# One GpSimd subtraction per pair of score rows instead of two, in a fused top-k attention and feed-forward kernel

## The chip, the core and the metric

The kernel runs on one core of a Trainium2 chip. A core has five engines with instruction streams of their own: TensorE (PE in the profile, with its weight loads as PEld), VectorE (DVE), ScalarE (ACT), GpSimd (POOL) and SyncE (SP, which here only issues transfers). Each works its stream in order, and semaphores tie the streams together. The metric is the device time of one execution in microseconds (us), as the median of several runs. Beside it stands one profiled execution, whose span and rows are those of the profile.

## The reference

Eight batches of eight heads, 576 positions, head size 64. Of each score row only the 32 largest entries are kept; the rest get no weight. The attention's output, as 4608 rows of 512, goes through a feed-forward pair of matrices with a leaky activation between them.

```python
scores = scale * np.matmul(q, k.transpose(0, 1, 3, 2))
kth = np.partition(scores, -top_k, axis=-1)[..., -top_k:-top_k + 1]   # top_k = 32
mask = scores >= kth
scores = np.where(mask, scores, -1000000000.0)
...
attn = np.exp(scores)
attn = attn / (np.sum(attn, axis=-1, keepdims=True) + 1e-09)
return np.matmul(attn, v).astype(np.float32)
...
h = x @ w_in
g = np.maximum(h, 0.0) + alpha * np.minimum(h, 0.0)
return (g @ w_out).astype(np.float32)
```

## The kernel before

Heads are taken two at a time, which makes 32 pairs of heads. The unit of the attention is a *duo*: two blocks of 128 score rows (one per head of a pair, or the last 64 positions of two pairs put together), so a tile of 128 partitions by 2 rows by 576 scores. There are 144 duos, 18 per batch. In this document a "row" of a duo is one of its two 576-wide halves.

A duo passes through these steps, each a function in the kernel:

- `st_qk` (PE) makes the scores in PSUM, and `st_exit` (ACT, one copy of 1152 elements) brings them to SBUF as the tile `s_sb`.
- `dve_slot` (DVE) takes the eight largest of each of six groups of 96 columns (`up`, `small`), and every second slot turns those of two duos into a bound for each row (`threshold_steps`, tiles `bot`, `neg`, `p`).
- `st_count` (ACT) computes for each of the two rows the sign of bound minus score (tile `sg`), and adds the signs up, which tells how many scores lie above the bound.
- `st_y` (POOL) multiplies scores by signs, one instruction of 576 elements per row (tile `y`). Scores above the bound change their sign, so the eight largest of `y` (DVE, `row`) are the candidates next below it. From the count and the candidates `pick_steps` (DVE) selects the 32nd largest score (`KT`, in tile `KZ`).
- `st_relu` (ACT and POOL) masks: ACT computes for each row Relu(2^60 x (kth - score)) into the tile `r`, which is zero where the score is kept and huge elsewhere, and POOL subtracts `r` from `s_sb` in place.
- `st_exp` (ACT, one instruction of 1152 elements, tile `w`) takes the exponential of both rows, and SP issues the transposing transfer to `wT`; `st_av` (PE) multiplies by the values; `norm_a` and `norm_b` (DVE) divide by the sum.

The feed-forward runs between these steps in small units (`h_pe`, `h_relu`, `o_pe`, `o_act`), and so do loads, the transposition of `q` and `k` on PE (copied out as `qkT` by ACT or DVE), and the casts of `v` on POOL (`cast_v`, tile `v`: two of 128x256 and one of 64x128 per pair of heads).

The order of each engine is written out by hand. The main loop has one *slot* per duo number n, and a table of lags says which duo each step takes in slot n: the count takes duo n-2, the mask duo n-4, Exp duo n-5, the values duo n-8 (from the thirteenth on n-7), the exit copy duo n+1. `Ordered` (line 21) keeps every engine's instructions in the order in which the loop makes them, apart from small DVE instructions. So in slot n ACT works: two Sign (duo n-2), Exp (duo n-5), sometimes a copy `o_sb` of a finished output, two Relu (duo n-4), the exit copy (duo n+1), sometimes a copy `qkT`. POOL works: two products `y` (duo n-2), two subtractions (duo n-4), sometimes a cast. The Exp of slot n+1 reads what slot n's subtractions wrote; the row maxima on DVE read what `y` wrote.

The tiles `sg` and `r` share a ring of three buffers, `s_sb` has six and `y` two. The first 140 duos are masked by `st_relu`; the last four use another way (`st_all`, `st_mask`) behind the loop, without a subtraction on POOL.

`st_relu` is called twice in a row, for rows 0 and 1, in the main loop (lines 744 to 746).

Of the kernel before, what the change touches and what calls it, by code (L numbers as in the profile page):

```python
# [12 lines left out]
ALU = mybir.AluOpType  # L13
# [46 lines left out]
def fast_path(tc, q, k, v, moe_w_in, moe_w_out, moe_alpha, out, flag):  # L60
# [11 lines left out]
    PE, ACT, DVE, POOL, SP = (  # L72
        Ordered(tc, e) for e in (nc.tensor, nc.scalar, nc.vector, nc.gpsimd, nc.sync)
    )
# [18 lines left out]
    with ExitStack() as ctx:  # L93
# [297 lines left out]
        def st_relu(n, i):  # L391
            s = T["s", n]
            if i == 0:
                T["r", n] = two.tile([128, 2, S], BF16, name="r", tag="sg", bufs=3)
            r = T["r", n]
            ACT.activation(r[:, i, :], s[:, i, :], AF.Relu, bias=KT[:, 2 * n + i:2 * n + i + 1], scale=-BIG)
            POOL.tensor_tensor(s[:, i, :], s[:, i, :], r[:, i, :], ALU.subtract)

        def st_exp(n):
            w = ws[n % 4]  # L400
# [313 lines left out]
        for n in range(ND):  # L714
# [29 lines left out]
            for m in duos_at("relu", n):  # L744
                st_relu(m, 0)
                st_relu(m, 1)
# [412 lines left out]
```

## Time and profile before

| what | value |
|---|---|
| median of 3 runs | 825.62 us (824.25 to 825.81) |
| the profiled execution's own time | 823.81 us |
| its span | 821.6 us |
| PE / DVE / ACT / POOL busy | 733.2 / 757.5 / 762.9 / 745.4 us |
| products `y` on POOL | 288, mean 1278 ns |
| subtractions on POOL | 280, mean 1277 ns |
| Relu `r` on ACT | 280, mean 769 ns |

A row of the groups reads: line, engine, operation, tile written and tiles read, shapes, count; then the busy time in us and the mean of one in ns; then the idle time of the engine just before these instructions and what ended it. Nearly all instructions carry line 32, the helper in `Ordered` that makes them, so the tiles name them. In rows in order of time the first number is the start in us from the span's start, the second the time from the first start to the last end of the instructions that the row merges (xcount); neighbours on one engine overlap at their ends, so starts stand a little closer than durations. A row of a window gives its bounds and length, the busy times of PE, PEld, DVE, ACT and POOL with their counts, then the granted TensorE clock, the share of the DMA engines and GB/s.

### The profile page before, as it was taken

How to read it: one execution, taken by the hardware profiler on the slowest of the kernel's cores; microseconds unless marked ns; L12 is line 12 of the kernel's file. 1: busy time of each engine (PE TensorE's matmuls, PEld its weight loads, DVE VectorE, ACT ScalarE, POOL GpSimd, SP SyncE). 2: the span in 40 equal slices, each digit the busy share in tenths (PEclk: the TensorE clock that was granted, in tenths of full speed). 3: DMA queues.
4: the chain of work that ended last, by engine and by line, in shares of the span. 5: the costliest groups of instructions: out<-in, count | busy, mean ns of one | idle time of the engine just before them, and what ended most of it. 6: DMA issues, size and time to landing. Idle time of an engine off the chain costs nothing.

```text
span 821.6 us, 17795 instructions
## 1 busy us (share of the span) xinstructions
PE 733.2 (89%) x5343; PEld 423.0 (51%) x5418; DVE 757.5 (92%) x3471; ACT 762.9 (93%) x1257; POOL 745.4 (91%) x701
## 2 busy tenths in 40 slices
PE   8888898989989899898989898898989899999886
PEld 5333444555545555455555454555545555565554
DVE  4999997999999999999999999999999999999951
ACT  4999997999999999999999999999999999999931
POOL 1899997999998999999999999999999998999920
PEclk9999998999999999999999999999999999999999
DMA  6699986556555656566566566566667654444461
GB/s 143 167 179 185 176 131 137 105 124 122 124 122 121 120 103 143 109 136 122 114 131 131 111 98 135 123 130 128 113 123 132 120 110 103 91 98 83 89 101 50
DMA packets 344328, 100.24 MB, mean 122 GB/s; under 512 B 338192, under 2 KB 338208, under 8 KB 344224
## 3 DMA queue, kind: packets, MB, share of 16 engines
q1 hardware_dynamic: 341152, 91.90, 57.1%
q0 software_dynamic: 1872, 6.82, 3.6%
q8 instruction: 45, 0.74, 0.4%
q14 instruction: 59, 0.48, 0.2%
q10 hardware_dynamic: 1200, 0.30, 0.2%
HBM read 36.71 MB, written 9.44 MB: 56 GB/s over the span
## 4 chain that ended last, share of the span: by engine, by line
DVE 46%; POOL 16%; PE 15%; ACT 15%; issue 5%; DMA 3%; SPq 0%; DVEq 0%; ACTq 0%; POOLq 0%
DVE small L32 14%; DVE p L32 12%; DVE up L32 8%; POOL y L32 8%; POOL s_sb L32 7%; DVE gT L32 5%; PE ps_sc L32 4%; ACT sg L32 4%; ACT r L32 4%; ACT s_sb L32 3%; PE pz L32 3%; PE ph L32 3%; ACT w L32 2%; DVE qkT L32 2%; PE xo L32 2%
## 5 line engine op out<-in xcount | busy, mean ns | idle before, releaser
L32 POOL TENSOR_TENSOR y<-s_sb,sg 128x576 f32<-128x576 f32 x288 | 362.6, 1278 | 33.5 <-ACT sg L32 33.1
L32 POOL TENSOR_TENSOR s_sb<-s_sb,r 128x576 f32<-128x576 f32 x280 | 352.1, 1277 | 7.6 <-ACT r L32 7.1
L32 ACT ACTIVATE sg<-s_sb,p 128x576 bf16<-128x576 f32 x288 | 221.3, 773 | 8.6 <-DVE p L32 7.1
L32 DVE MAX8 up<-s_sb 128x8 f32<-128x96 f32 x864 | 213.4, 247 | 10.1 <-ACT s_sb L32 10.1
L32 DVE MAX8 p<-y 128x8 f32<-128x576 f32 x288 | 215.4, 749 | 6.5 <-POOL y L32 5.8
L32 DVE MAX8 small<-s_sb 128x8 f32<-128x96 f32 x864 | 217.6, 252 | 0.0
L32 PE MATMUL ps_sc<-qkT 64*128 64x512 f32 (+2 forms) x768 | 185.2, 572 | 18.8 <-ACT s_sb L32 18.7
L32 ACT ACTIVATE r<-s_sb,KZ 128x576 bf16<-128x576 f32 x280 | 201.0, 769 | 0.3 <-DVE KZ L32 0.3
L32 ACT COPY s_sb<-ps_sc 128x1152 f32<-128x1152 f32 x144 | 159.0, 1104 | 12.8 <-PE ps_sc L32 12.3
L32 ACT ACTIVATE w<-s_sb 128x1152 bf16<-128x1152 f32 x140 | 161.7, 1155 | 1.0 <-POOL s_sb L32 0.8
L32 PE MATMUL ph<-xT,w_in_b 128*128 128x256 bf16 (+1 forms) x1472 | 151.4, 251 | 5.9 <-ACT qkT L32 2.8
L32 PEld LDWEIGHTS <-w_in_b 128*128 128x128 bf16 x1472 | 120.6, 98 | 49.2 <-issue 10.4
L32 PE MATMUL pz<-w_out_b,gT 128*128 128x512 bf16 x517 | 134.6, 379 | 8.1 <-issue 6.3
L32 PE MATMUL xo<-v,wT 128*128 128x65 bf16 (+1 forms) x1560 | 123.8, 199 | 5.6 <-DMA wT<-w 3.9
L32 PEld LDWEIGHTS <-wT 128*128 128x128 bf16 (+3 forms) x1600 | 97.9, 100 | 39.7 <-DMA wT<-w 8.6
L32 DVE TENSOR_SCALAR gT<-ph 128x512 bf16<-128x512 f32 x136 | 91.9, 676 | 11.4 <-PE ph L32 11.4
L32 PEld LDWEIGHTS <-gT 128*128 128x128 bf16 x576 | 55.8, 98 | 69.8 <-issue 14.6
L32 PEld LDWEIGHTS ps_sc<-kd,qkT 128*128 128x128 f32 x256 | 38.5, 190 | 99.6 <-issue 96.1
L32 PEld LDWEIGHTS ps_sc<-qkT 64*128 64x128 f32 (+1 forms) x768 | 55.8, 170 | 62.7 <-issue 29.3
L32 PE MATMUL ps_sc<-kd,qkT 128*128 128x128 f32 x256 | 63.1, 329 | 1.1 <-DMA kd<-qkT 1.1
L32 PE MATMUL rest<-idle 128*128 128x512 bf16 x196 | 49.8, 380 | 7.3 <-DVE gT L32 5.4
L32 ACT ACTIVATION_READ_ACCUMULATOR sg<-s_sb,p 128x1 f32 x288 | 55.7, 194 | 0.0
(66 smaller groups left out, 580.0 us busy)
## 6 DMA issues: line engine op xcount, KB each, us to landing
k_st<-in_k_dram SPq DMA_DIRECT2D x64, 128.0 KB, 2.9
v_st<-in_v_dram SPq DMA_DIRECT2D x64, 128.0 KB, 2.7
q_st<-in_q_dram SPq DMA_DIRECT2D x62, 128.0 KB, 2.8
out_dram<-o_sb SPq DMA_DIRECT2D x31, 256.0 KB, 2.5
w_st<-in_moe_w_out_dram POOLq DMA_DIRECT2D x4, 1024.0 KB, 6.8
wT<-w SPq DMA_TRANSPOSE x144, 3.5
w_in_b<-in_moe_w_in_dram POOLq DMA_DIRECT2D x4, 512.0 KB, 6.5
k_st<-in_k_dram SPq DMA_DIRECT2D x32, 32.0 KB, 2.5
```

What stands on the lines that cost most here:

```text
L32: ins = self.tc.keep_in_program_order(f(*a, **kw))
```

## The change

Both Relu stay as they are. The subtraction is no longer issued once for each row but once behind the second Relu, over the whole tile of 128 x 2 x 576, which is contiguous and so one run of 1152 elements per partition. It reads what both Relu wrote and stands in POOL's order where the second subtraction stood. The products `y` remain one instruction per row, and the lags stay.

```diff
         def st_relu(n, i):
...
             ACT.activation(r[:, i, :], s[:, i, :], AF.Relu, bias=KT[:, 2 * n + i:2 * n + i + 1], scale=-BIG)
-            POOL.tensor_tensor(s[:, i, :], s[:, i, :], r[:, i, :], ALU.subtract)
+            if i:
+                POOL.tensor_tensor(s, s, r, ALU.subtract)
```

## The prediction

> **What bounds the kernel now.** I read the page first (busy shares, groups, the shares of the chain of waits), then the table of waits, then one stretch of 18 slots as a window, then the instructions of that stretch in order of time.
>
> ```profile
> span 821.6 us, 17795 instructions
> PE 733.2 (89%) x5343; PEld 423.0 (51%) x5418; DVE 757.5 (92%) x3471; ACT 762.9 (93%) x1257; POOL 745.4 (91%) x701
> DVE 46%; POOL 16%; PE 15%; ACT 15%; issue 5%; DMA 3%; SPq 0%; DVEq 0%; ACTq 0%; POOLq 0%
> L32 POOL TENSOR_TENSOR y<-s_sb,sg 128x576 f32<-128x576 f32 x288 | 362.6, 1278 | 33.5 <-ACT sg L32 33.1
> L32 POOL TENSOR_TENSOR s_sb<-s_sb,r 128x576 f32<-128x576 f32 x280 | 352.1, 1277 | 7.6 <-ACT r L32 7.1
> ```
>
> Four engines lie between 89 and 93% busy and the chain is spread over all of them, so no engine alone is the bound. The subtraction (280 times, 1277 ns) waited 7.1 us in all for ACT's Relu.
>
> ```profile
> 517.63:610.97 93.34, 84.11 (x605) 48.98 (x612) 92.39 (x431) 93.00 (x154) 92.87 (x85) 1.00 0.61 122
> ```
>
> This is a stretch of 18 slots, from one slot's subtraction to the same place 18 slots on. Busy times are PE, weight load, DVE, ACT, POOL: of 93.34 us ACT is idle 0.34, POOL 0.47, DVE 0.95. Whatever makes one of the three wait in this stretch has almost nothing to hide in, and the granted TensorE clock (1.00) is whole.
>
> ```profile
> ACT w L32 <- POOL s_sb L32: 0.8, 3, 0.5
> DVE p L32 <- POOL y L32: 5.8, 11, 1.2
> ```
>
> So far ACT's Exp (`w`) has almost never waited for the subtraction: 0.8 us, three times.
>
> The loop that matters runs over two engines. ACT works through Exp of duo n-5, perhaps a copy `o_sb`, two Relu of duo n-4, the exit copy of duo n+1, perhaps a copy `qkT`, two Sign of the next slot, next Exp. That next Exp needs this slot's subtraction. A slot with no extra copy, on ACT:
>
> ```profile
> 525.72 1.15 ACT L32 ACTIVATE w<-s_sb 128x1152 bf16<-128x1152 f32 x1
> 526.77 1.42 ACT L32 ACTIVATE r<-s_sb,KZ 128x576 bf16<-128x576 f32 x2
> 528.11 1.09 ACT L32 COPY s_sb<-ps_sc 128x1152 f32<-128x1152 f32 x1
> 529.11 0.77 ACT L32 ACTIVATE sg<-s_sb,p 128x576 bf16<-128x576 f32 x1
> ...
> 530.63 1.15 ACT L32 ACTIVATE w<-s_sb 128x1152 bf16<-128x1152 f32 x1
> ```
>
> Exp to Exp is 4.91 us. The second Relu ends 2.47 us after Exp began (526.77 + 1.42 - 525.72), and 2.44 us of ACT work follow before the next Exp. The first Relu ends some 0.67 us ahead of the second (1.42 less its own 0.77, which is how far two starts stand apart). POOL in the same time:
>
> ```profile
> 522.81 2.51 POOL L32 TENSOR_TENSOR s_sb<-s_sb,r 128x576 f32<-128x576 f32 x2
> 525.28 2.50 POOL L32 TENSOR_TENSOR y<-s_sb,sg 128x576 f32<-128x576 f32 x2
> 527.75 2.51 POOL L32 TENSOR_TENSOR s_sb<-s_sb,r 128x576 f32<-128x576 f32 x2
> 530.21 0.39 POOL L32 CAST v<-v_st 128x256 bf16<-128x256 f32 x1
> 530.57 2.52 POOL L32 TENSOR_TENSOR y<-s_sb,sg 128x576 f32<-128x576 f32 x2
> ...
> 540.80 0.28 POOL L32 CAST v<-v_st 64x128 bf16<-64x128 f32 x1
> 541.05 2.51 POOL L32 TENSOR_TENSOR y<-s_sb,sg 128x576 f32<-128x576 f32 x2
> ```
>
> A pair takes 2.47 us from start to start and 2.51 to its own end; a large cast adds 0.36, a small one 0.25. The subtraction at 527.75 starts 0.44 us before the second Relu ends (528.19). That head start is what the change forbids.
>
> **The change, part by part.** 140 pairs of subtractions become 140 single ones of 1152 elements on POOL, at the place of the second; PE, DVE, ACT and SP keep their work and order, and no DMA moves.
>
> *The wait it adds.* The one instruction needs both Relu, so it starts at the later of the end of `y` and the second Relu's end. Behind it on POOL stand the casts and the next `y`, for which DVE's row maxima wait; ACT's Exp waits for the subtraction itself, and behind Exp everything on ACT. The two semaphore delays show where one engine did stand waiting:
>
> ```profile
> 552.62 0.57 ACT L32 COPY o_sb<-pz 128x512 f32<-128x512 f32 x1
> 553.08 1.45 ACT L32 ACTIVATE r<-s_sb,KZ 128x576 bf16<-128x576 f32 x2
> 553.95 2.52 POOL L32 TENSOR_TENSOR s_sb<-s_sb,r 128x576 f32<-128x576 f32 x2 [0.41 <-ACT r L32]
> ...
> 422.78 2.51 POOL L32 TENSOR_TENSOR s_sb<-s_sb,r 128x576 f32<-128x576 f32 x2
> 425.32 1.16 ACT L32 ACTIVATE w<-s_sb 128x1152 bf16<-128x1152 f32 x1 [0.16 <-POOL s_sb L32]
> ```
>
> The first Relu of 553.08 ends near 553.86 and the subtraction begins 0.08 to 0.09 later (I use 0.08); a subtraction ending at 425.29 lets Exp begin 0.03 later. `o_sb` adds 0.46 us between Exp and Relu (552.62 to 553.08).
>
> *What it saves.* One start less per duo. Its fixed price is not in the trace for this shape. From below: nothing. The nearest row for a flat operation is memset on POOL:
>
> ```profile
> 1.25 0.93 POOL L32 MEMSET kd<- 128x128 f32 x6
> 2.91 0.47 POOL L32 MEMSET v<- 128x10 bf16 x8
> ...
> L32 POOL MEMSET kd<- 128x128 f32 x6 | 0.9, 204 | 0.0
> L32 POOL MEMSET v<- 128x10 bf16 x8 | 0.5, 173 | 0.0
> ...
> L32 POOL CAST v<-v_st 128x256 bf16<-128x256 f32 x8 | 3.2, 398 | 0.0
> L32 POOL CAST v<-v_st 64x128 bf16<-64x128 f32 x4 | 1.2, 290 | 0.0
> L32 ACT COPY qkT<-tps 128x512 f32<-128x512 f32 x4 | 2.3, 584 | 0.0
> L32 ACT COPY o_sb<-pz 128x512 f32<-128x512 f32 x4 | 2.3, 568 | 0.0
> ```
>
> Without the last one's own time, memsets of 128 elements start (0.93 - 0.20) / 5 = 0.15 us apart and those of 10 elements (0.47 - 0.17) / 7 = 0.04 apart: nearly all of the 0.04 is fixed. From above, the casts: 0.36 for 256 elements and 0.25 for 128 leave 0.25 - 128 x 0.11/128 = 0.14 fixed, with an access pattern of several levels. The subtraction is flat, like the memset, so I take 0.04: the merged instruction holds POOL 2.43 us and ends 2.47 after its start.
>
> A rule of the Trainium skill bears on this term. "GPSIMD Engine Reference", section 3.1, gives 4497 ns for a two-input operation of 2048 elements and a floor of about 2.5 cycles per element at 1.2 GHz. By that floor (an estimate) 576 elements are 1.20 us and the spacing seen leaves 0.04 to save; by the 4497 ns and the 1277 of our row, 2.19 ns an element, merged 2.54 us against 2.51: a loss of about 0.02 a duo, and a total about 6 us higher than mine. No run here shows which.
>
> *The sum.* The rows just quoted also count the extras in those 18 slots: 8 large casts, 4 small, 4 `qkT`, 4 `o_sb`. With the rules above a subtraction starts at the later of
>
> - POOL: last start + 2.43 + cast + 2.47, which is 4.90 bare, 5.15 with a small, 5.26 with a large cast;
> - ACT: Exp + 2.47 + 0.08 (+ 0.46 with `o_sb`), where Exp starts 2.47 + 0.03 after the last subtraction began. That is 5.05 bare and 5.51 with `o_sb`. A `qkT` copy (0.58, some 0.48 between starts) makes ACT's own round 4.91 + 0.48 = 5.39 and may set Exp instead.
>
> Carried through the 18 slots in their order (casts and copies as their times place them), the steps are 5.15, 5.29, 5.26, 5.51, 5.15, 5.29, 5.51, 5.05, 5.26, 5.26, 5.15, 5.51, 5.26, 5.26, 5.51, 5.05, 5.26, 5.26: 94.99 us against 93.34 now, so +1.65. (5.29 is the step after a `qkT` copy where ACT leads: 2.50 + 5.39 + 2.55 less the 5.15 before it.) Seen by class: a bare slot goes from ACT's 4.91 to 5.05, and a cast, until now absorbed because POOL could run ahead, is paid in full.
>
> ```profile
> L32 POOL TENSOR_TENSOR s_sb<-s_sb,r 128x576 f32<-128x576 f32 x236 | 296.7, 1277 | 6.3 <-ACT r L32 6.0
> L32 POOL TENSOR_TENSOR y<-s_sb,sg 128x576 f32<-128x576 f32 x235 | 295.3, 1276 | 7.1 <-ACT sg L32 6.9
> ```
>
> From 159.8 us to the end of the slots there are 236 subtractions, 118 duos, 6.56 such stretches: 6.56 x 1.65 = +10.8 us. The 22 duos before I count at nothing: there POOL's `y` waited 33.1 - 6.9 = 26 us for Sign, and a start that is late anyway costs no more; if that cover were absent they would add 22/18 x 1.65 = 2 us. The last four duos have no subtraction. The profiled execution took 823.81 us (2.2 beyond its span), so it goes to 834.6; the median of the runs, 825.62, stands 1.8 above that execution, and I forecast 836.4 for the median.
>
> **The rivals.** (a) *No fixed price is saved*, so POOL runs 1152 elements in twice the time of 576. 16 of the 18 steps contain the subtraction: 16 x 0.04 = 0.64 more, 2.29 x 6.56 = +15.0, that is 840.6. For it: the ends of neighbours overlap already. Against: the memsets.
>
> (b) *Covered.* The fixed price is that of the casts, 0.14: 16 x 0.10 = 1.6 less, 0.05 x 6.56 = +0.3, 825.9, no change. For it: they are POOL compute too. Against: their pattern.
>
> (c) *Faster.* Above about 0.14 us a duo POOL no longer sets a step and the saving wins: ACT's idle 0.34 us per stretch could go, 0.34 x 6.56 = 2.2 us, 823.4. For it: POOL is 92.87 of 93.34 busy. Against: no flat row has such a price, and ACT at 93.00 leaves no more to gain.
>
> (d) *DVE loses too.* `y` starts later after each wait; DVE's maximum already waited for `y` 11 times (5.8 us). If each of the 118 duos lost a further 0.05 us, 6 us are added: 842.3.
>
> **How the numbers follow.** My forecast 0.60, (a) 0.20, (d) 0.07, (b) 0.08, (c) 0.05. Faster by over 0.2% is (c), within 0.2% (about what a measurement of this kernel can tell from no change) is (b), slower is the rest. The range goes from 829, where the saving is about 0.11, up to 842.5, past (a) and to (d).
>
> **What would show it.** In the profile after: 140 subtractions of 128x1152 of about 2.47 us, starting 2.43 before the next POOL instruction; POOL's wait for Relu grown from 7.1 to some 25 us (0.15 to 0.6 each in slots without a cast); ACT's Exp waiting for the subtraction in bare, cast and `o_sb` slots, 0.14 and more each; 18 slots near 95 us; busy times of ACT and DVE unchanged. The forecast is wrong if the merged instruction takes under 2.37 us, if Exp's waits do not appear, or if the step of a slot with a cast stays below 5.2.

## The result: slower by 0.4%

The changed kernel takes 827.36 us (median of 17 runs, 826.01 to 830.48) beside 824.25 us before (823.18 to 827.98, 17 runs; the 825.62 from which the forecast started was the median of the first three): a ratio of 1.004, 95% interval 1.003 to 1.005, or about 3 us. The forecast was slower by 10.8, with a range of 829 to 842.5. The profiled execution took 828.2 us.

The page of the changed kernel and its table of waits:

```profile
span 826.0 us, 17655 instructions
PE 735.3 (89%) x5343; PEld 423.7 (51%) x5418; DVE 759.6 (92%) x3471; ACT 768.3 (93%) x1257; POOL 727.4 (88%) x561
DVE 26%; ACT 25%; PE 24%; POOL 11%; issue 10%; DMA 4%; SPq 0%; ACTq 0%; POOLq 0%
L32 POOL TENSOR_TENSOR y<-s_sb,sg 128x576 f32<-128x576 f32 x288 | 362.7, 1280 | 28.2 <-ACT sg L32 27.6
L32 POOL TENSOR_TENSOR s_sb<-s_sb,r 128x1152 f32<-128x1152 f32 x140 | 332.5, 2375 | 35.1 <-ACT r L32 29.0
...
POOL s_sb L32 <- ACT r L32: 29.0, 46, 1.1
DVE p L32 <- POOL y L32: 9.3, 24, 1.2
ACT sg L32 <- DVE p L32: 7.2, 17, 1.0
```

POOL's work shrank by 18 us (745.4 to 727.4), and its wait for Relu grew from 7.1 to 29.0. One merged subtraction takes 2375 ns against the pair's 2.51 us. DVE's row maxima (`p`) now wait for `y` 24 times and 9.3 us instead of 11 times and 5.8. The stretch of 18 slots that took 93.34 us (the tight stretch from here on):

```profile
520.69:615.00 94.31, 84.24 (x602) 48.80 (x609) 92.73 (x431) 93.64 (x153) 90.63 (x67) 1.00 0.60 120
```

It is 0.97 us longer; 1.65 was forecast. Between starts of subtractions, the six groups of 18 slots from slot 22 to slot 130 are longer by 0.31, 0.62, 0.99, 1.35, 0.97 and 0.40 (the fourth has a granted clock of 0.98 here, all others 1.00).

The idle column hides part of ACT's waiting. In the kernel before, Exp starts 0.09 us after the start of the accumulator read ahead of it (530.54 to 530.63), while that read still runs to 530.73. Here, in order of time on ACT of the changed kernel:

```profile
522.79 0.19 ACT L32 ACTIVATION_READ_ACCUMULATOR sg<-s_sb,p 128x1 f32 x1
523.10 1.16 ACT L32 ACTIVATE w<-s_sb 128x1152 bf16<-128x1152 f32 x1
```

Exp came 0.22 us late (0.31 instead of 0.09), and only half of that counts as idle. So I also compared starts, in the trace of each kernel (e1, e8 and e13 are experiments below): for each pair of neighbouring instructions of the same kind, the time between their starts less the 10th percentile for that pair, summed from 159.8 to 778 us:

| us | before | after | e1, wait alone | e8, Exp freed | e13, bound first |
|---|---|---|---|---|---|
| ACT: Exp late | 0.8 | 5.9 | 19.6 | 0.0 | 6.9 |
| ACT: Sign late | 11.9 | 11.0 | 6.0 | 16.7 | 5.2 |
| DVE: row maximum late | 1.1 | 6.1 | 15.1 | 6.7 | 0.6 |

At first sight this is the forecast's picture: Exp loses 5.1 us and the last subtraction starts 5.1 us later (775.98 to 781.11). But the table of waits also has another chain, from POOL's `y` over DVE to Sign. In order of time, in the changed kernel:

```profile
520.77 0.76 DVE L32 MAX8 p<-y 128x8 f32<-128x576 f32 x1 [0.40 <-POOL y L32]
...
527.05 0.17 DVE L32 TENSOR_SCALAR p<-small 128x4 f32<-128x4 f32 x1
...
527.25 0.78 ACT L32 ACTIVATE sg<-s_sb,p 128x576 bf16<-128x576 f32 x1 [0.17 <-DVE p L32]
...
531.34 2.38 POOL L32 TENSOR_TENSOR s_sb<-s_sb,r 128x1152 f32<-128x1152 f32 x1 [0.63 <-ACT r L32]
```

Between 159.8 and 778 us, DVE's maxima show no idle wait for `y` in the kernel before; here they wait 13 times and 3.7 us. The experiments separate the two chains.

### The profile page after: what moved, and what is told of

Its sections match the earlier page's. It is cut to its first block, busy times and chain, and to the rows that moved or that the text cites. A ratio compares the mean times of both kernels' runs of the same rounds, so it can differ in the third digit from the quotient of the medians.

```text
span 826.0 us, 17655 instructions
## 1 busy us (share of the span) xinstructions
PE 735.3 (89%) x5343; PEld 423.7 (51%) x5418; DVE 759.6 (92%) x3471; ACT 768.3 (93%) x1257; POOL 727.4 (88%) x561
## 4 chain that ended last, share of the span: by engine, by line
DVE 26%; ACT 25%; PE 24%; POOL 11%; issue 10%; DMA 4%; SPq 0%; ACTq 0%; POOLq 0%
DVE small L32 8%; PE ps_sc L32 7%; ACT r L32 7%; ACT sg L32 6%; POOL y L32 6%; DVE p L32 6%; ACT s_sb L32 5%; PE pz L32 5%; DVE up L32 5%; PE ph L32 4%; POOL s_sb L32 4%; PE xo L32 3%; ACT w L32 3%; DVE gT L32 3%; DMA wT<-w 1%
## 5 line engine op out<-in xcount | busy, mean ns | idle before, releaser
L32 POOL TENSOR_TENSOR s_sb<-s_sb,r 128x1152 f32<-128x1152 f32 x140 | 332.5, 2375 | 35.1 <-ACT r L32 29.0
L32 ACT COPY s_sb<-ps_sc 128x1152 f32<-128x1152 f32 x144 | 158.6, 1101 | 12.1 <-PE ps_sc L32 11.9
```

The lines of the kernel that those rows point to most:

```text
L32: ins = self.tc.keep_in_program_order(f(*a, **kw))
```

## The experiments

**e4, the fixed price of one start.** Four duos with subtractions halved, four merged, the rest as before.

```diff
-            POOL.tensor_tensor(s[:, i, :], s[:, i, :], r[:, i, :], ALU.subtract)
+            if 60 <= n < 64:
+                for c in (0, S // 2):
+                    POOL.tensor_tensor(s[:, i, c:c + S // 2], s[:, i, c:c + S // 2], r[:, i, c:c + S // 2], ALU.subtract)
+            elif 80 <= n < 84:
+                if i:
+                    POOL.tensor_tensor(s, s, r, ALU.subtract)
+            else:
+                POOL.tensor_tensor(s[:, i, :], s[:, i, :], r[:, i, :], ALU.subtract)
```

> The kernel before, with the subtractions of four duos split into halves of 288 and those of four others merged to 1152: the fixed price of one start in one trace. A line through 1277 ns at 576 and 2375 at 1152 has 1.91 ns per element and 0.18 us fixed (0.14 from start to start), so 288 should take 730 ns. If the fixed price is the 0.04 of my forecast, and 2375 came from elsewhere, 288 should take about 660.

The groups of its profile, and one merged subtraction with what follows it in order of time:

```profile
L32 POOL TENSOR_TENSOR s_sb<-s_sb,r 128x576 f32<-128x576 f32 x264 | 332.1, 1279 | 6.7 <-ACT r L32 6.2
L32 POOL TENSOR_TENSOR s_sb<-s_sb,r 128x288 f32<-128x288 f32 x16 | 11.2, 738 | 0.1
L32 POOL TENSOR_TENSOR s_sb<-s_sb,r 128x1152 f32<-128x1152 f32 x4 | 9.5, 2372 | 1.1 <-ACT r L32 1.1
...
466.20 2.37 POOL L32 TENSOR_TENSOR s_sb<-s_sb,r 128x1152 f32<-128x1152 f32 x1 [1.11 <-ACT r L32]
468.52 0.40 POOL L32 CAST v<-v_st 128x256 bf16<-128x256 f32 x1
```

738, 1279 and 2372 ns lie on a line of 1.88 to 1.90 ns per element with 0.19 us fixed. From start to next start the merged one takes 2.32 (466.20 to 468.52) against 2.47 for a pair: the change saves 0.15 us of POOL per duo, not 0.04. The price is that of the casts, which I had kept for the other end of the range. The one run took 824.04 us, like before.

**e1, the new wait without the saving.**

```diff
-                POOL.tensor_tensor(s, s, r, ALU.subtract)
+                for j in (1, 0):
+                    POOL.tensor_tensor(s[:, j, :], s[:, j, :], r[:, j, :], ALU.subtract)
```

> Both subtractions stay 576 wide, but POOL takes row 1 ahead of row 0, so that neither starts before the second Relu: the wait of the change alone, without its saving. Theory W (the new wait costs what the step-by-step sum gave without any saving, and 0.14 us saved per duo pays most of it back): 2.29 us per 18 slots, +15 us, near 840. Rival M (the wait is covered, and what the change costs comes from the long instruction itself): no more than 1 us above before.

835.97 us against 823.73, ratio 1.0141 (1.0117 to 1.0166): +12 us. The wait is far from covered, and the merged instruction pays most of it back; rival M is out. The 12 is less than 15: the tight stretch grew by 2.71 us (93.34 to 96.05), more than the 2.29 expected, while the groups of slots 22 to 40, 40 to 58 and 112 to 130 grew by 1.47, 1.95 and 1.45. The stretch that I multiplied was among the tightest.

**e2 and e3, Exp behind both Relu** (without and with the merged subtraction), meant to give Exp slack.

```diff
-            for m in duos_at("exp", n):
-                st_exp(m)
             run(n, "lin_out")
...
                 st_relu(m, 1)
+            for m in duos_at("exp", n):
+                st_exp(m)
```

> The kernel before with one swap: on ACT the Exp stands behind the two Relu instead of ahead of them, so that the subtraction has about 2 us more before Exp needs it. Theory W: nothing waits there in the kernel before (0.8 us), so nothing is gained, 0 to -2 us. Rival P (the Relu, 1.1 us earlier now, must wait for DVE's picks in every second slot): slower by 70 x 0.1 = 7 us or more.

> The changed kernel with the same swap: one subtraction per duo, but Exp does not need it until one round of ACT later. Theory W: Exp's waits for the subtraction go, ACT runs its own round (4.91 us bare), and the loss of the change disappears: 822 to 825 where before is 824.3. Rival M: the loss stays, 827 or more.

839.0 and 838.42 us, ratios 1.0182 (1.0161 to 1.0203) and 1.0165 (1.0144 to 1.0186): the move itself costs about 15 us, so nothing can be read of the wait, except that the two kernels end alike. Relu waits 6.6 us for DVE's pick in e2, as rival P had it, which is less than half of the 15. In e3, in order of time on ACT:

```profile
562.72 1.15 ACT L32 ACTIVATE w<-s_sb 128x1152 bf16<-128x1152 f32 x1
563.90 1.12 ACT L32 COPY s_sb<-ps_sc 128x1152 f32<-128x1152 f32 x1
```

The exit copy starts 0.03 us after Exp's end (563.87), where ACT's neighbours elsewhere start some 0.10 before the end. Those 0.13 us times 138 such slots are 18 us. The copy takes over the `s_sb` buffer that this Exp frees; that this is the reason is argued, not shown, but the next runs fit it.

**e5, e6 and e7, Exp between the two Relu,** so that a Relu lies between Exp and the copy: merged, before, and with the late pair of e1.

```diff
                 st_relu(m, 0)
+            for m in duos_at("exp", n):
+                st_exp(m)
+            for m in duos_at("relu", n):
                 st_relu(m, 1)
```

> The changed kernel with ACT's Exp between the two Relu: Exp comes 0.67 us later, behind the first Relu, and still keeps 0.67 of Relu between itself and the exit copy that takes over its buffer. Theory W (Exp's wait for the merged subtraction is what the change costs): from the second Relu's end to the next Exp ACT now has 2.44 + 0.67 = 3.1 us of other work against 0.08 + 2.375 + 0.03 = 2.49 on POOL, so the wait goes, a bare slot returns to ACT's 4.91, and with 0.155 us less POOL work per duo the time is that of before or up to 2 us less: 822 to 824.5. Rival M: the loss of 3 us stays, 827 or more. Rival P (the first Relu, 1.1 us earlier, waits for DVE's pick as in the run with Exp behind both, 6.6 us there): 2 to 7 us above before.

> The kernel before with the same move of Exp and its two subtractions: the control of the move itself. Theory W: Exp does not wait in the kernel before, so nothing is gained, 0 to -1 us. Rival P: 2 to 7 us slower.

> The wait alone (two subtractions of 576, row 1 first, both behind the second Relu) with Exp between the Relu. Theory W: the start is as late as in the run with the wait alone (+12 us there), but Exp has 3.1 us for 0.08 + 2.51 + 0.03 = 2.62, so most of the 12 us goes, within 3 us of the control of the move. If instead the late start costs through POOL's own row of work (casts paid in full, DVE's maxima late), 6 us or more stay.

e5 took 835.68 us, ratio 1.0135 (1.0086 to 1.0184); e6 829.43, 1.0054 (1.0030 to 1.0078); e7 839.91, 1.0188 (1.0134 to 1.0241). The control costs only 5 us now instead of 15. The table of waits has 8.5 us of ACT's Relu waiting for DVE's pick in e6 and 10.9 in e5, as rival P had it:

```profile
ACT r L32 <- DVE KZ L32: 8.5, 22, 0.9
```

```profile
ACT r L32 <- DVE KZ L32: 10.9, 29, 0.9
```

Exp does not wait for POOL in any of the three. Yet the merged kernel is about 6 us above its control (835.68 to 829.43, though the six runs of e5 spread from 831.01 to 841.37) and the late pair 10 us (839.91 to 829.43). Theory W had both within 3. Relu's longer wait for the pick accounts for 2.4 of the 6 us by these tables; the rest must have a way past Exp.

**e8, e9 and e10, Exp freed of POOL with every instruction in its place.** The subtractions write into `r`, so that Exp reads the unmasked scores.

```diff
-                POOL.tensor_tensor(s, s, r, ALU.subtract)
+                POOL.tensor_tensor(r, s, r, ALU.subtract)
```

> The changed kernel with the merged subtraction's result written into r instead of s: the mask is left out of the output, every instruction stays in its place, and ACT's Exp no longer waits for POOL. Theory W (the loss goes through Exp's wait): the 5 us that Exp loses in the changed kernel between 160 and 778 us go, and the time is within 1 us of the control (two subtractions into r) or below it, 821 to 825. Rival D (the loss goes through POOL: y late, DVE's maxima late, ACT's Sign late): 2 us or more above the control stay.

> The wait alone (two subtractions of 576, row 1 first, behind the second Relu) with the results in r, the mask left out of the output and Exp free of POOL. Theory W: of the 12 us that this wait cost, at most 2 stay above the control. Rival D: 5 us or more stay, since POOL still starts late and has no saving.

> The control for the two others: the kernel before with its subtractions' results in r, the mask left out of the output. Exp waited 0.8 us for POOL in the kernel before, so both theories expect no change: 823 to 825.

The control e10 is at 823.56 us, ratio 0.9991 (0.9978 to 1.0004), no change. e8 is at 828.08, 1.0049 (1.0036 to 1.0062), and e9 at 832.0, 1.0102 (1.0088 to 1.0117). Without any Exp waiting, the merged kernel still loses 4.5 us, all of it; of the late pair's 12, some 8 stay. Theory W falls for the change itself: Exp's wait is not needed for the loss. What replaced it stands in the tables of waits, first of e8, then of e10:

```profile
ACT sg L32 <- DVE p L32: 12.3, 27, 1.1
DVE p L32 <- POOL y L32: 9.9, 24, 1.2
```

```profile
ACT sg L32 <- DVE p L32: 7.9, 17, 1.0
DVE p L32 <- POOL y L32: 5.7, 11, 1.2
```

One turn of it in e8 in order of time, on POOL, DVE and ACT:

```profile
518.64 2.51 POOL L32 TENSOR_TENSOR y<-s_sb,sg 128x576 f32<-128x576 f32 x2
...
521.18 0.76 DVE L32 MAX8 p<-y 128x8 f32<-128x576 f32 x1 [0.40 <-POOL y L32]
...
526.30 0.76 DVE L32 MAX8 p<-y 128x8 f32<-128x576 f32 x1
526.97 0.46 DVE L32 MAX8 small<-neg 128x8 f32<-128x31 f32 x4
527.47 0.17 DVE L32 TENSOR_SCALAR p<-small 128x4 f32<-128x4 f32 x1
...
527.67 0.78 ACT L32 ACTIVATE sg<-s_sb,p 128x576 bf16<-128x576 f32 x1 [0.54 <-DVE p L32]
...
530.26 1.42 ACT L32 ACTIVATE r<-s_sb,KZ 128x576 bf16<-128x576 f32 x2
...
531.82 2.37 POOL L32 TENSOR_TENSOR r<-s_sb,r 128x1152 bf16<-128x1152 f32 x1 [0.70 <-ACT r L32]
```

`y` ends at 521.15 and the row maximum begins at 521.18, after 0.40 us of idling. DVE then runs with no gap above 0.04 us, with a maximum ahead of the bound, to the bound at 527.64. Sign, which needs the bound, begins at 527.67, 0.54 late; the Relu follow late, and POOL waits 0.70 for the second.

**e11 and e12, DVE's maxima freed as well.** On top of e8 and e10 the row maxima read `s` instead of `y`.

```diff
-            DVE.max(out=T["p9", d // 2][:, 2 * (d % 2) + i, 1:9], in_=T["y", d][:, i, :])
+            DVE.max(out=T["p9", d // 2][:, 2 * (d % 2) + i, 1:9], in_=T["s", d][:, i, :])
```

> The merged subtraction's result goes into r (the mask left out of the output), and DVE's row maxima read s instead of y (so the threshold picked and the output are wrong): neither Exp nor the maxima wait for POOL any more, all instructions stay. Theory D (the late start reaches the time through y, DVE's maxima, the bound p behind them and ACT's Sign): the 4 us above the control that stayed with Exp alone freed go, within 1 us of the control of this pair or below. If they stay, 3 us or more, the loss has another way still.

> The control for that: two subtractions into r (the mask left out), maxima over s instead of y (threshold and output wrong). DVE waited 5.8 us for y in the kernel before, little of it on the path: 0 to -3 us against before.

819.4 and 819.67 us, ratios 0.9947 (0.9929 to 0.9965) and 0.9947 (0.9916 to 0.9978). With both ways cut, one subtraction and two take the same time, and Sign's wait for the bound is the same, in e11 and in e12:

```profile
POOL r L32 <- ACT r L32: 27.2, 49, 1.2
ACT sg L32 <- DVE p L32: 6.7, 12, 1.0
```

```profile
ACT sg L32 <- DVE p L32: 6.7, 12, 1.0
POOL r L32 <- ACT r L32: 6.0, 17, 0.4
```

POOL waits 21 us longer for Relu in e11, and that costs nothing. No third way shows, within the 2 to 3 us that the intervals leave; the tight stretch takes 92.94 and 93.03 us. The maxima freed while Exp still waits, the fourth case, was not run; the next pair comes nearest to it.

**e13 and e14, the bound finished ahead of the row maximum,** in kernels that compute everything.

```diff
                 negate()
+                least()
+                turn()
             else:
                 h_relu()
             for d in rows:
                 row(d, 0)
-            if turn:
-                least()
-                turn()
```

> The changed kernel with one DVE move: in every second slot the bound p is finished (least and turn) ahead of the first row maximum instead of behind it, so that Sign no longer hangs on a maximum that waits for y. Theory D: Sign's waits for p shrink by up to 0.67 us each where they stand, the change's 3 to 4 us come back, 821 to 825. Rival: DVE's own chain from neg to least has no other work between, 72 slots x 0.1 = 7 us more on a DVE that has little idle time, 828 or more.

> The kernel before with the same DVE move, the control of the move: Sign waits less for p (7.1 us in 14 times in the kernel before), 0 to -4 us; by the rival up to +7.

e13, the merged kernel, takes 824.05 us, ratio 0.9996 (0.9979 to 1.0014): the loss is gone. e14, the control, takes 824.08, 1.0002 (0.9978 to 1.0025): by itself the move gives nothing. Waits of e13, then of e14:

```profile
POOL s_sb L32 <- ACT r L32: 28.9, 48, 1.1
DVE p L32 <- POOL y L32: 4.7, 10, 1.2
ACT sg L32 <- DVE p L32: 2.6, 6, 0.8
```

```profile
ACT sg L32 <- DVE p L32: 6.0, 17, 0.8
DVE p L32 <- POOL y L32: 4.8, 10, 1.2
```

POOL waits as in the changed kernel (28.9 against 29.0) and Exp is even a little later (6.9 us in the table above), but Sign's wait falls from 7.2 to 2.6 us and DVE's from 9.3 to 4.7. So the link between DVE's bound and Sign carries the loss of the change.

The medians of e13 and e14 leave some 2 us either way, and their profiled executions differ (824.08 and 821.45), so I compared the groups of 18 slots too. In the first five, from slot 22 to 112, e13 is 0.5 us longer than e14 in all, where the changed kernel was 4.2 longer than the one before. In the sixth it is 1.70 longer; there e13's granted clock is 0.98 and, behind the dip, the exit copy waits 1.6 us for PE's scores, while e14 has 1.00. The move is not free either: the tight stretch takes 93.88 us in e13 and 93.80 in e14, against 93.34 before, and both win it back elsewhere, 0.8 us of it in the group from slot 22. So in the tight stretch itself the two kernels are all but equal, and both slower than before. No version tried that computes everything beats the kernel before.

## Why the prediction was wrong

The direction was right, and so was the wait: POOL stands for the second Relu 29 us (I had said some 25), Exp waits in slots of the kinds that I named (by starts, 63 times by 0.04 to 0.07 us and 12 times by 0.17 to 0.23, not by 0.14 and more each), and the instructions of ACT and DVE take what they took (ACT's mean durations are within 1%, though its busy time is 5.4 us longer). The size was wrong, 3 us for 10.8, below the range. Of my own signs of a wrong forecast, one came true, a slot with a large cast at 5.15, below 5.2; the merged instruction, 2.375 us, stands at the edge of another, 2.37. Step by step:

- *What it saves.* This is the term that failed. I took 0.04 us per duo from memset, because it is flat, and it is 0.15: the casts were the better neighbour. The rule that I drew from the Trainium skill ("GPSIMD Engine Reference"; the 4497 ns stand in section 3.1, the floor in section 2.1) leaned the same wrong way: its floor of about 2.5 cycles per element at 1.2 GHz is 2.08 ns, and the run shows 1.88 to 1.90 ns (about 2.3 cycles) with one f32 and one bf16 input, so more of each instruction is fixed. Its other figure, from which I worked out 2.19 ns per element and a loss of 0.02 per duo, does not fit this operation either. Here the measurement decides.
- *The sum with the right price.* Without rounding, POOL takes 2.321 us from the merged start to the next and 2.375 to its end. The time from Exp to the second Relu's end is 2.492 (2.488 before; my 2.47 was read from one slot). My two rules then give 4.98 for a bare slot, 5.04 and 5.15 with a cast, 5.45 with `o_sb` (0.47 more), 10.37 for the two slots around a `qkT` copy: 4 x 10.37 + 2 x 4.98 + 5.04 + 3 x 5.15 + 4 x 5.45 = 93.73, which is +0.39, or +2.6 over 6.56 stretches. So the wrong price made most of the miss. In the trace, 15 of the 18 steps of the tight stretch lie within 0.02 us of these rules. The other three are 0.55 longer in all, which makes up nearly all the rest of the 0.97: steps such as 531.34 - 525.73 = 5.61, where the rules give 5.33. Each stands behind a Sign that began 0.03 us after DVE's bound was done (527.25, 569.17 and 579.32), which is in neither rule. That +2.6 comes near the median is thus partly luck.
- *The multiplication by 6.56* took one of the tightest stretches for all; e1 has 12 us where it gives 15. The 22 duos that I counted at nothing did cost nothing: the first subtraction behind them starts at 159.36 us, against 159.87 before.
- *The path.* I wrote that ACT's Exp carries the wait into the time, and put DVE's maxima into a rival (d) with 7 in 100. The loss goes when (d)'s link is relieved (e13), and not when Exp is freed (e8): late `y`, late maximum, late bound, late Sign. Rival (d)'s size, 6 us on top of mine, was wrong too. Exp's waits lie beside Sign's: taken away, Sign waits longer by about as much (11.0 to 16.7 us by starts). Where the start is late without any saving, freeing Exp does bring back some 4 of 12 us.
- *Rival (b)* had the right price but for 0.01. Its +0.3 us lacked the 0.02 at Relu and the late Sign. *Rival (c)* said that above 0.14 the saving wins. The price is above, yet the kernel is slower: a bare slot still takes 4.98 us instead of 4.91, because Exp, the two Relu and the subtraction now follow one another in a ring: 2.49 + 0.08 + 2.38 + 0.03.

What stays open: how e9's remaining 8 us divide; whether Exp's waits alone, with the maxima freed, would cost anything; and why the move of the bound lengthens the tight stretch of the kernel before, where Sign's wait in all fell only from 7.1 to 6.0 us.

## What to carry to other kernels

For the fixed price of an instruction take the row nearest in what the engine does (read, compute, write), and best two sizes of the same operation; a flat memset was a poor stand-in. Where several engines are 99% busy, as ACT, POOL and DVE in the tight stretch, follow a new wait through every reader of the late engine: the one that stands in the table of the delayed instruction's own reader need not be the one that decides. And before multiplying a stretch, compare it with its neighbours.

## What the hardware showed that I had not expected

A two-input operation on POOL costs 0.15 us per start from start to start, while memsets of ten elements stood 0.04 apart and casts left 0.14: the price depends on the kind of instruction. And a wait of under 0.1 us on ACT shows as no idle time at all, since neighbours overlap by that much: in the changed kernel the groups give Exp 1.4 us of idle time in all, where the starts show 5.9 us late between 160 and 778 us.
